# First-layer sums of the 7-product scheme kept in PSUM, GpSimd sums of weights and tokens issued steps ahead of ScalarE's copies, and the PSUM split of the balancing stage changed

## The chip, the cores and the metric

The kernel runs on one core of a Trainium2 chip. The metric is device time of one execution in microseconds (us); several executions are timed and their median is quoted. Engine names: PE is TensorE, DVE is VectorE, ACT is ScalarE, POOL is GpSimd, SP is SyncE, which issues the DMAs.

## What is computed

Three stages follow each other on 2304 tokens of 512 values (4 batches of 576), all in fp32:

```python
p_packed = sm_attn(p, k, v)              # 32 packed rows for each of 8 heads
x = sm_attn(q, p_packed, p_packed)       # 4 x 576 tokens, 512 wide
P = exp(x @ w_gate - max)                # 8 experts
for _ in range(8):                       # balancing
    P /= P.sum(1); P /= P.sum(0); P *= N / E
out = sum over e of P[:, e] * (relu(x @ w1[e]) @ w2[e])      # d_ff 1024
r = relu(out @ w_in); result = (s * r * r + b) @ w_out       # d_ff 2048
```

## The kernel before

**Precision.** PE multiplies in the fp32r format. Each operand is kept as a high part, rounded to fp32r, and a low part, the rest; a product takes three passes (high by high, high by low, low by high). Whatever feeds PE is therefore made twice: ACT casts or copies the high part, and DVE or POOL subtracts it from the full value to get the low part.

**Units.** The eight experts' first layers are cut into 32 units `u` of 256 hidden columns. Since the tokens are `x = a2 * ppf` (attention weights by packed values), the first layer is applied as `z = ppf * w1` (`zmm`, 64 small PE products a unit) and then `x`-sided weights by `z`. Units 0 to 4 run in the plain way: `mm1a` makes 288 tokens by 128 hidden columns with 6 PE matmuls of 288 columns, ACT takes the relu as the high part, DVE the low part, and `tile2` (line 478, six matmuls of 128x512 for a tile of 128 tokens) makes the second layer in a PSUM bank, which DVE weighs and adds to `acc` (line 493). The balancing iterations (`balance`) are woven between the slots of units 0 to 3 and need PSUM banks of their own. After them ACT weighs what lies in `acc` already (`gated`, line 484).

**7-product units.** Units 5 to 29 (25 of them, four batches `b` each, so 100 slots; `slotw`) compute the four blocks of a 2x2 block product with seven block products instead of eight (`mm1w`, `product`; each product is three matmuls of 288 columns into a PSUM bank). A slot uses three banks of the pool "h", which has four: `ps_a` collects products 1, 6, 5, 3 one on top of the other, `ps_b` takes product 2, `ps_e` products 7 and 4. After products 1, 6 and 5 ACT copies what `ps_a` holds to SBUF (`snap`, line 425); DVE adds a bank to such a copy (`plus`, line 428, in place in SBUF); ACT takes the relu of the sum (line 416) and DVE subtracts it for the low part of `h` (`h_put`, line 417). Between the jobs `j1` to `j4` stand the second-layer tiles of the slot before: five in slots b=0 and b=2, four in b=1 and b=3.

**What the products need.** `z_whole(u+1)` makes the next unit's `z` with 64 PE matmuls into all four banks of the pool "y", and ACT copies them to `zp` (line 374). For each batch `z_split` has POOL form four sums (line 384), ACT cast two pieces to `zz` (line 386) and POOL make their low parts (line 387). `x_sums` does the like for the tokens, once for each batch, while unit 4 runs: POOL adds high and low part to `px` (line 394), forms four differences `tp` (line 397), ACT casts them to `xt` (line 398), and POOL makes the low part (line 399). `px` and `tp` take the two buffers of the pool "w", in which the second-layer weights also lie (`load_w2`, line 116 the low part).

**Order.** Behind the attention stage, instructions are not issued as the program is written: the framework's scheduler reorders them on each engine by a cost model of its own, within the dependences and buffer counts. Where a side job is called decides only roughly where its instructions land. The lines of calls are `side` lists, in `slotw` and in the loop over `u` and `b`.

**PSUM.** Eight banks. From the end of the attention stage on, the kernel before has y=4 and h=4; balancing sums and `z` take "y" banks.

Of the kernel before, what the change touches and what calls it, by code (L numbers as in the profile page):

```python
# [25 lines left out]
HB = S // 2  # L26
# [16 lines left out]
def tile_kernel(ctx: ExitStack, tc: tile.TileContext, qT, kT, vv, pb, w1c, w2c, wcat64, wg, sv, bv, out):  # L43
# [301 lines left out]
    def zmm(u, pr, qs=(0, 1), tags="mm"):  # L345

        w = wts[1, u]
        ps = [psa(t, "ps_z") for t in tags]
        for q in qs:
            for r, c, rows, cols in heads():  # L350
                mmul(ps[r][cols, q * FU:(q + 1) * FU], ppf[rows, 2 * pr + q, cols], w[rows, c, :],  # L351
                     start=True, stop=True)
        return ps

    def zput(u, pr, ps, qs=(0, 1)):
        if (u, pr) not in zs:
# [20 lines left out]
    def z_split(u, b):  # L377

        src = zplain[0][:, b // 2, :, b % 2, :]
        zz = zq_[u, b] = z_p.tile([128, 2, 7, 128], F32R, tag="z", name="zz")  # L380
        sums = wt_p[-1].tile([128, 4, 128], F32, tag="sums", name="sums")
        for n, (x_, y_, op) in enumerate(((src[:, 0], src[:, 2], ALU.add), (sums[:, 0], src[:, 1], ALU.subtract),
                                          (src[:, 1], src[:, 0], ALU.subtract), (src[:, 3], sums[:, 1], ALU.subtract))):
            G.tensor_tensor(out=sums[:, n], in0=x_, in1=y_, op=op)  # L384
        for o, s_ in ((slice(0, 3), src[:, 1:4]), (slice(3, 7), sums)):
# [3 lines left out]
    def x_sums(b):  # L389

        o = slice(b * S, (b + 1) * S)
        px = w_p.tile([128, 2048], F32, tag="w", name="px")[:, :2 * S].rearrange("p (c t) -> p c t", c=2)
        tp = w_p.tile([128, 2048], F32, tag="w", name="tp")[:, :4 * HB].rearrange("p (n t) -> p n t", n=4)
        G.tensor_tensor(out=px, in0=xa[0][:, :, o].bitcast(F32), in1=xa[1][:, :, o].bitcast(F32), op=ALU.add)
        x11, x12, x21, x22 = px[:, 0, :HB], px[:, 0, HB:], px[:, 1, :HB], px[:, 1, HB:]
        for n, (x_, y_) in enumerate(((x12, x11), (x22, tp[:, 0]), (x22, x12), (x21, tp[:, 1]))):
            G.tensor_tensor(out=tp[:, n], in0=x_, in1=y_, op=ALU.subtract)  # L397
        A.copy(xt[0][:, b, 0], tp)
        G.tensor_tensor(out=xt[0][:, b, 1], in0=tp, in1=xt[0][:, b, 0].bitcast(F32), op=ALU.subtract)  # L399

    LEFT = {1: 0, 4: 1, 2: 2, 5: 3, 6: 4, 7: 5, 3: 6}

    def product(n, u, b, p_, start=False):

        o = b * S
        for m, (k, a) in enumerate(PASSES):
            x_ = {1: lambda: xa[k][:, 0, o:o + HB], 2: lambda: xa[k][:, 1, o:o + HB],
                  3: lambda: xa[k][:, 1, o + HB:o + S], 4: lambda: xt[0][:, b, k, 3],
                  5: lambda: xt[0][:, b, k, 0], 6: lambda: xt[0][:, b, k, 1], 7: lambda: xt[0][:, b, k, 2]}[n]()
            mmul(p_[:, :HB], zq_[u, b][:, a, LEFT[n], :], x_, start=start and m == 0, stop=m == 2,  # L410
                 skip_group_check=True)

    def h_put(b, f, t, s_):
        o = (b % 2) * S + t * HB
        hh, hl = (h[:, f, k, o:o + HB] for k in range(2))
        A.activation(out=hh, in_=s_, func=AF.Relu)  # L416
        V.scalar_tensor_tensor(out=hl, in0=s_, scalar=0.0, in1=hh.bitcast(F32), op0=ALU.max, op1=ALU.subtract)  # L417

    def mm1w(u, b):

        p, s_ = {}, {}

        def snap(n):
            s_[n] = wt_p[-1].tile([128, HB], F32, tag=f"snap{n}", name="snap")
            A.copy(s_[n], p["a"][:, :HB])  # L425

        def plus(n, bank):
            V.tensor_tensor(out=s_[n], in0=p[bank][:, :HB], in1=s_[n], op=ALU.add)  # L428

        def j1():  # L430
            p["a"], p["b"] = psa("h", "ps_a"), psa("h", "ps_b")
            product(1, u, b, p["a"], True)
            snap(1)
            product(2, u, b, p["b"], True)
            plus(1, "b")
            h_put(b, 1, 0, s_[1])

        def j2():
            p["e"] = psa("h", "ps_e")
            product(6, u, b, p["a"])  # L440
            snap(2)
            product(7, u, b, p["e"], True)

        def j3():
            product(5, u, b, p["a"])
            snap(3)
            plus(3, "e")
# [133 lines left out]
    def slotw(u, b, side=()):  # L581
# [37 lines left out]
    with tc.tile_pool(name="ppf", bufs=1) as ppf_p, tc.tile_pool(name="w1p", bufs=2) as w1_, ExitStack() as start:  # L619
# [3 lines left out]
        with tc.manual_schedule(), tc.tile_pool(name="at", bufs=1) as at_p, ExitStack() as early:  # L623
# [114 lines left out]
            for s in range(1, B - 1):  # L738
# [17 lines left out]
        share(ctx, y=4, h=4)  # L756
        banks.pop("m")
        order = [(u, 1, q) for u in range(UP) for q in (2, 3)]
        order += [(u, pr, q) for u in range(UP, W0) for pr in range(2) for q in range(4)]
        cut = order.index((UE, 0, 1))  # L760
        with tc.tile_pool(name="mid", bufs=1) as mid:
            bal = balance(mid)
            for u, pr, q in order[:cut]:
                side = []
                if u >= UP:
                    side = side1(u, pr, q)
                elif u == UP - 1:
                    side = zjobs(UP) if q == 2 else []
                elif q == 2:
                    side = [lambda: list(load_w2(UP))]  # L770
                slot1(u, pr, q, side + [nxt(bal)])
            for _ in bal:
                pass
        start.close()
        with tc.tile_pool(name="wt", bufs=1) as wt:
            wt_p.append(wt)
            xt.append(wt.tile([128, B, 2, 4, HB], F32R, name="xt"))
            for n, (u, pr, q) in enumerate(order[cut:]):
                side = side1(u, pr, q)
                if n < B:  # L780
                    side.append(lambda b=n: x_sums(b))
                if (pr, q) == (1, 0):
                    side.insert(0, lambda: z_whole(W0))
                if (pr, q) == (1, 2):
                    side.append(lambda: z_split(W0, 0))
                slot1(u, pr, q, side)
            for u in range(W0, W9):
                for b in range(B):
                    side = []
                    if b < B - 1:  # L790
                        side.append(lambda u=u, b=b: z_split(u, b + 1))
                    if b == 0:
                        side.append(lambda u=u: list(load_w2(u + 1)))
                    if b == B - 1:
                        if u + 1 < W9:
                            side += [lambda u=u: z_whole(u + 1), lambda u=u: z_split(u + 1, 0)]
                        else:
                            side += zjobs(u + 1)
                        side.append(lambda u=u: load_w1(u + 2))
# [78 lines left out]
```

## Time and profile before

| | |
|---|---|
| median of three timed runs | 1824.58 us (1822.94 to 1825.3) |
| the profiled execution: own time, span of its trace | 1825.6 us, 1823.8 us |
| busy: PE, DVE, ACT, POOL | 94%, 69%, 40%, 38% |
| mean granted TensorE clock | 0.991 of full speed |
| 7-product units | 286 to 1324 us of the span |
| the second model (two matrices and the squared relu) | from about 1410 us |

The profile is of one execution. A row of a timeline gives the start, the duration, the engine, the line, the operation with its output and inputs, and in brackets how long the engine had been idle before and what ended that. A "waits" row sums such idle time by what ended it. Matmuls are pipelined, so the modelled ends of neighbouring rows overlap. For what an engine's delay costs, the starts of repeated instructions are safer than the idle time.

### The profile page before, as it was taken

Reading aid. Unit: us, or ns where it says so; the run is one execution under the profiler, and the core shown is the slowest. Engines: PE = TensorE matmul, PEld = TensorE weight load, DVE = VectorE, ACT = ScalarE, POOL = GpSimd, SP = SyncE. Lnnn points to the kernel's source line nnn. Section 1 sums busy time; section 2 is a strip of 40 time slices with the busy share of each in tenths; the row PEclk is TensorE's granted clock in tenths of the full one; section 3 lists DMA queues with packets and bytes.
Section 4 is the critical chain, followed back from the end, with each engine's and each line's share of the span. In section 5 each row is a group of like instructions: output and inputs, shape, how many; then the busy total and the mean of one; then the engine's idle time right before and its main releaser. Section 6 shows DMA issues by size and latency. Waiting matters only on the chain.

```text
span 1823.8 us, 28626 instructions
## 1 busy us (share of the span) xinstructions
PE 1720.6 (94%) x11227; PEld 1455.6 (80%) x11227; DVE 1253.1 (69%) x2374; ACT 728.8 (40%) x1609; POOL 689.6 (38%) x847
## 2 busy tenths in 40 slices
PE   7999969999999999999999999999999999999999
PEld 4778858777777777777777777777888898999998
DVE  4745726666666666666666666666798679988874
ACT  4542333444444444444444444444423432222221
POOL 0330083444444444444444444444210233333332
PEclk9999979999999999999999999999999999999999
DMA  9420010100001000010000010001010011111102
GB/s 276 129 59 24 13 32 16 35 24 24 24 24 36 24 24 24 24 36 24 24 24 24 25 34 24 24 24 35 2 47 24 24 35 47 36 47 37 45 12 105
DMA packets 37400, 71.59 MB, mean 39 GB/s; under 512 B 3216, under 2 KB 24720, under 8 KB 37264
## 3 DMA queue, kind: packets, MB, share of 16 engines
q1 hardware_dynamic: 37264, 69.76, 13.3%
q8 instruction: 88, 1.44, 0.3%
q14 instruction: 48, 0.39, 0.1%
HBM read 65.03 MB, written 4.72 MB: 38 GB/s over the span
## 4 chain that ended last, share of the span: by engine, by line
PE 79%; DVE 9%; POOL 5%; ACT 4%; issue 2%; DMA 1%; SPq 0%; POOLq 0%; DVEq 0%; ACTq 0%
PE ps L478 50%; PE ps L505 10%; PE ps_a L410 7%; PE ps L464 4%; PE ps_e L410 4%; DVE h L417 3%; POOL sums L384 3%; DVE acc L493 2%; ACT zp L374 2%; PE ps_z L351 2%; PE ps_b L410 1%; ACT zz L386 1%; POOL tp L397 1%; DMA q__115<-qT 1%; POOL xt L399 0%
## 5 line engine op out<-in xcount | busy, mean ns | idle before, releaser
L478 PE MATMUL ps<-w,h 128*128 128x512 f32 x4296 | 1102.5, 396 | 44.9 <-DVE h L417 25.3
L478 PEld LDWEIGHTS ps<-w,h 128*128 128x128 f32 x4296 | 775.7, 189 | 199.9 <-DVE h L417 39.6
L493 DVE SCALAR_TENSOR_TENSOR acc<-ps,pm,acc 128x512 f32<-128x512 f32 x504 | 376.6, 747 | 204.3 <-PE ps L478 201.2
L417 DVE SCALAR_TENSOR_TENSOR h<-snap,h 128x288 fp32r<-128x288 f32 x300 | 225.8, 753 | 90.3 <-ACT h L416 90.3
L425 ACT COPY snap<-ps_a 128x288 f32<-128x288 f32 x300 | 120.1, 400 | 247.8 <-PE ps_a L410 245.2
L384 POOL TENSOR_TENSOR sums<-zp 128x128 f32<-128x128 f32 x200 | 93.1, 486 | 318.4 <-ACT zp L374 312.5
L416 ACT ACTIVATE h<-snap 128x288 fp32r<-128x288 f32 x300 | 133.8, 446 | 188.6 <-DVE snap L428 185.0
L387 POOL TENSOR_TENSOR zz<-zp,zz 128x384 fp32r<-128x384 f32 x100 | 102.3, 1023 | 234.3 <-ACT zz L386 234.3
L515 POOL TENSOR_TENSOR h<-g,h 128x384 fp32r<-128x384 f32 x96 | 98.5, 1026 | 221.7 <-ACT h L514 219.5
L410 PEld LDWEIGHTS ps_a<-xt,zz 128*128 128x128 f32 x600 | 100.2, 188 | 73.2 <-ACT snap L425 45.6
L410 PE MATMUL ps_a<-xt,zz 128*128 128x288 f32 x600 | 124.7, 303 | 35.4 <-ACT snap L425 35.4
L505 PE MATMUL ps<-xa,w 128*128 128x384 f32 x576 | 146.9, 336 | 0.0
L505 PE MATMUL ps<-xb,w 128*128 128x384 f32 x576 | 146.9, 335 | 0.0
L387 POOL TENSOR_TENSOR zz<-sums,zz 128x512 fp32r<-128x512 f32 x100 | 129.0, 1290 | 0.0
L428 DVE TENSOR_TENSOR snap<-ps_e,snap 128x288 f32<-128x288 f32 x200 | 90.3, 452 | 47.5 <-ACT snap L425 43.6
L410 PEld LDWEIGHTS ps_a<-xa,zz 128*128 128x128 f32 x600 | 101.6, 189 | 16.3
L464 PE MATMUL ps<-xa,z 128*128 128x288 f32 x672 | 111.7, 304 | 2.7 <-ACT xa L274 1.9
L464 PEld LDWEIGHTS ps<-xa,z 128*128 128x128 f32 x672 | 101.3, 193 | 15.3 <-ACT xa L274 3.6
L410 PE MATMUL ps_a<-xa,zz 128*128 128x288 f32 x600 | 112.4, 296 | 0.0
L410 PE MATMUL ps_e<-xt,zz 128*128 128x288 f32 x600 | 112.4, 296 | 0.0
L514 ACT CAST h<-g 128x384 fp32r<-128x384 f32 x96 | 49.4, 515 | 149.6 <-DVE g L513 149.6
L505 PEld LDWEIGHTS ps<-xa,w 128*128 128x128 f32 x576 | 105.0, 188 | 3.7
(209 smaller groups left out, 1920.8 us busy)
## 6 DMA issues: line engine op xcount, KB each, us to landing
raw<-w2c SPq DMA_DIRECT2D x32, 512.0 KB, 3.7
raw<-wcat SPq DMA_DIRECT2D x32, 512.0 KB, 3.6
acc<-kT SPq DMA_DIRECT2D x8, 576.0 KB, 8.5
out<-acc SPq DMA_DIRECT2D x18, 256.0 KB, 2.0
acc<-vv SPq DMA_DIRECT2D x5, 576.0 KB, 9.8
q__113<-qT SPq DMA_DIRECT2D x1, 576.0 KB, 10.6
q__115<-qT SPq DMA_DIRECT2D x1, 576.0 KB, 12.4
v__157<-vv SPq DMA_DIRECT2D x1, 576.0 KB, 12.9
```

The costliest lines, as they stand in the source:

```text
L384: G.tensor_tensor(out=sums[:, n], in0=x_, in1=y_, op=op)
L387: G.tensor_tensor(out=zz[:, 1, o], in0=s_, in1=zz[:, 0, o].bitcast(F32), op=ALU.subtract)
L410: mmul(p_[:, :HB], zq_[u, b][:, a, LEFT[n], :], x_, start=start and m == 0, stop=m == 2, skip_group_check=True)
L416: A.activation(out=hh, in_=s_, func=AF.Relu)
L417: V.scalar_tensor_tensor(out=hl, in0=s_, scalar=0.0, in1=hh.bitcast(F32), op0=ALU.max, op1=ALU.subtract)
L425: A.copy(s_[n], p["a"][:, :HB])
L428: V.tensor_tensor(out=s_[n], in0=p[bank][:, :HB], in1=s_[n], op=ALU.add)
L464: mmul(p_[:, :HB], z[:, a, q // 2, i, f * 128:(f + 1) * 128], xa[k][:, i, t], start=(n + i == 0), stop=(n + i == 3))
L478: mmul(y, h[:, f, a, hc:hc + 128], ws[f][k], start=(n == 0), stop=(n == 3 * UF - 1))
L493: V.scalar_tensor_tensor(out=a, in0=y, scalar=pm[:, T, u // UE:u // UE + 1], in1=a, op0=ALU.mult, op1=ALU.add)
L505: mmul(p, w[:, a, c * 128:(c + 1) * 128], x_part(k, c)[:, b * BLK:(b + 1) * BLK], start=(n == 0), stop=(n == 3 * NC - 1))
L515: G.tensor_tensor(out=hl, in0=g, in1=hh.bitcast(F32), op=ALU.subtract)
```

## The change

It has four parts.

1. `plus` writes its sum to PSUM: in `j1` onto `ps_b`, in `j3` the sum of `ps_e` and the copy goes to `ps_b`, in `j4` onto `ps_e`. `h_put` reads the bank, on ACT and on DVE. Each sum is the same.
2. `z_split` is divided: `z_add` (POOL's four sums) is called a slot ahead of `z_split`, which only casts and makes the low parts. `z_whole(u+1)` and the loads of weights move from slot b=3: `z_whole` behind the last job of b=2, `load_w2` to b=1.
3. `x_sums` is divided into `x_add` and `x_split`, the differences are formed in place in one "w" buffer, and the four batches are spread over unit 4 and the first two 7-product slots.
4. While balancing, the banks are y=3, h=2, m=3, where balancing sums and some of `z` have "m"; y=4, h=4 come behind it.

The core of the diff:

```diff
+    def z_add(u, b):
         src = zplain[0][:, b // 2, :, b % 2, :]
-        zz = zq_[u, b] = z_p.tile([128, 2, 7, 128], F32R, tag="z", name="zz")
         sums = wt_p[-1].tile([128, 4, 128], F32, tag="sums", name="sums")
...
+        z_sums[u, b] = [(slice(0, 3), src[:, 1:4]), (slice(3, 7), sums)]
+    def z_split(u, b):
+        zz = zq_[u, b] = z_p.tile([128, 2, 7, 128], F32R, tag="z", name="zz")
+        for o, s_ in z_sums[u, b]:
             A.copy(zz[:, 0, o], s_)
             G.tensor_tensor(out=zz[:, 1, o], in0=s_, in1=zz[:, 0, o].bitcast(F32), op=ALU.subtract)
...
-        px = w_p.tile([128, 2048], F32, tag="w", name="px")[:, :2 * S].rearrange("p (c t) -> p c t", c=2)
-        tp = w_p.tile([128, 2048], F32, tag="w", name="tp")[:, :4 * HB].rearrange("p (n t) -> p n t", n=4)
...
+        for out_, x_, y_ in ((x11, x12, x11), (x12, x22, x12), (x22, x22, x11), (x21, x21, x22)):
+            G.tensor_tensor(out=out_, in0=x_, in1=y_, op=ALU.subtract)
...
-    def h_put(b, f, t, s_):
+    def h_put(b, f, t, p_):
+        s_ = p_[:, :HB]
...
-        def plus(n, bank):
-            V.tensor_tensor(out=s_[n], in0=p[bank][:, :HB], in1=s_[n], op=ALU.add)
+        def plus(n, bank, to):
+            V.tensor_tensor(out=p[to][:, :HB], in0=p[bank][:, :HB], in1=s_[n], op=ALU.add)
...
-            plus(1, "b")
-            h_put(b, 1, 0, s_[1])
+            plus(1, "b", "b")
+            h_put(b, 1, 0, p["b"])
...
-            plus(3, "e")
-            h_put(b, 0, 1, s_[3])
+            plus(3, "e", "b")
+            h_put(b, 0, 1, p["b"])
...
-            plus(2, "e")
-            h_put(b, 0, 0, s_[2])
+            plus(2, "e", "e")
+            h_put(b, 0, 0, p["e"])
...
+            share(start, y=3, h=2, m=3)
             bal = balance(mid)
...
+        banks.pop("m")
+        share(ctx, y=4, h=4)
...
+            early = {(0, 1): [(x_add, 0)], (0, 3): [(x_split, 0)], (1, 0): [(x_add, 1), (z_whole, W0)],
+                     (1, 1): [(z_add, W0, 0)], (1, 2): [(x_split, 1), (z_split, W0, 0)],
+                     (1, 3): [(z_add, W0, 1), (x_add, 2)]}
...
+                    if b == 2:
+                        side[3].append((z_whole, u + 1) if u + 1 < W9 else (zrun, u + 1))
```

What the scheduler makes of it is shown at three places. First PE at a unit's change, before (u=14 to 15): `ps_2` are second-layer tiles, `zz_7487` belongs to batch b=3 of the old unit, `ps_z` are the matmuls of `z_whole`, of which one row of 64 is kept at each end.

```order
L478 MATMUL ps_2_7549<-w_6938,h_73 128x512 x6
L410 MATMUL ps_a_7557<-xa0_70,zz_7487 128x288 x2
...
L410 MATMUL ps_b_7558<-xa0_70,zz_7487 128x288 x2
...
L478 MATMUL ps_2_7570<-w_6938,h_73 128x512 x6
L351 MATMUL ps_z_7579<-w1__7265,ppf_86 32x256
...
L410 MATMUL ps_a_7557<-xt_2576,zz_7487 128x288 x3
L410 MATMUL ps_e_7619<-xt_2576,zz_7487 128x288 x3
```

and with the change (`zz_7500` is batch b=3 here):

```order
L491 MATMUL ps_2_7549<-w_7037,h_73 128x512 x6
L351 MATMUL ps_z_7558<-w1__7252,ppf_86 32x256
...
L491 MATMUL ps_2_7598<-w_7037,h_73 128x512 x6
L422 MATMUL ps_a_7606<-xa0_70,zz_7500 128x288 x2
...
L422 MATMUL ps_b_7607<-xa0_70,zz_7500 128x288 x2
...
L491 MATMUL ps_2_7619<-w_7037,h_73 128x512 x6
L422 MATMUL ps_a_7606<-xt_2588,zz_7500 128x288 x3
```

Before, product 6 (the second into `ps_a`, from `xt`) follows `z` at once; now a tile, products 1 and 2 and another tile stand between `z` and product 6.

Second, ACT at the same place, before and with the change. `zp` are the copies of `z`, `zz` the casts (the second needs POOL's sums), `snap` the copies of `ps_a`.

```order
L374 COPY zp_7578<-ps_z_7579 128x2x2x128
L374 COPY zp_7578<-ps_z_7580 128x2x2x128
L386 CAST zz_7636<-zp_7578 128x384
L386 CAST zz_7636<-sums_7637 128x512
L374 COPY zp_7578<-ps_z_7597 128x2x2x128
L374 COPY zp_7578<-ps_z_7598 128x2x2x128
L425 COPY snap_7623<-ps_a_7557 128x288
L425 COPY snap_7649<-ps_a_7557 128x288
L416 ACTIVATE h_73<-snap_7649 128x288
```

```order
L374 COPY zp_7557<-ps_z_7558 128x2x2x128
L374 COPY zp_7557<-ps_z_7559 128x2x2x128
L392 CAST zz_7668<-zp_7557 128x384
L392 CAST zz_7668<-sums_7627 128x512
L374 COPY zp_7557<-ps_z_7576 128x2x2x128
L374 COPY zp_7557<-ps_z_7577 128x2x2x128
L438 COPY snap_7611<-ps_a_7606 128x288
L429 ACTIVATE h_73<-ps_b_7607 128x288
L438 COPY snap_7636<-ps_a_7606 128x288
```

ACT's order is the same up to the first `snap`: four copies and two casts. That first `snap` was the one behind product 6 and is now the one behind product 1.

Third, ACT at the end of the balancing stage, before and with the change: `acc` is the weighing of line 484 (497 with the change), `xt` the cast of a batch's token differences, `h` relus of unit 4.

```order
L484 ACTIVATE acc_72<-acc_72,pm_78 128x512 x5
L467 ACTIVATE h_73<-ps_1_2577 128x288
L398 CAST xt_2576<-tp_2601 128x1152
L467 ACTIVATE h_73<-ps_1_2609 128x288
L398 CAST xt_2576<-tp_2637 128x1152
L467 ACTIVATE h_73<-ps_1_2627 128x288
L467 ACTIVATE h_73<-ps_1_2654 128x288
L398 CAST xt_2576<-tp_2682 128x1152
```

```order
L410 CAST xt_2588<-px_2612 128x1152
...
L410 CAST xt_2588<-px_2719 128x1152
L497 ACTIVATE acc_72<-acc_72,pm_78 128x512 x3
L480 ACTIVATE h_73<-ps_1_2589 128x288
L497 ACTIVATE acc_72<-acc_72,pm_78 128x512 x3
L480 ACTIVATE h_73<-ps_1_2618 128x288
L497 ACTIVATE acc_72<-acc_72,pm_78 128x512
L410 CAST xt_2588<-px_2912 128x1152
L410 CAST xt_2588<-px_3016 128x1152
L480 ACTIVATE h_73<-ps_1_2636 128x288
```

The casts of the first two batches now stand between weighings, and those of the last two directly behind each other, still ahead of relus of unit 4.

## Rows read from the trace of the kernel before

**Rows 1.** The page, busy time, share of the span and instructions of each engine.

```profile
PE 1720.6 (94%) x11227; PEld 1455.6 (80%) x11227; DVE 1253.1 (69%) x2374; ACT 728.8 (40%) x1609; POOL 689.6 (38%) x847
```

**Rows 2.** What PE waited for, 286 to 1324 us: total, times, longest (us).

```profile
PE ps_a L410 <- ACT snap L425: 35.4, 24, 1.8
PE ps L478 <- DVE h L417: 25.3, 50, 0.7
```

**Rows 3.** Timeline of PE, 582 to 624 us: start, duration, operation, [idle before].

```profile
584.77 0.55 PE L410 MATMUL ps_a<-xa,zz 128*128 128x288 f32 x3
...
593.08 0.56 PE L410 MATMUL ps_a<-xa,zz 128*128 128x288 f32 x3
...
593.87 0.62 PE L478 MATMUL ps<-w,h 128*128 128x512 f32 x2
...
595.12 1.21 PE L478 MATMUL ps<-w,h 128*128 128x512 f32 x4 [0.50 <-DVE h L417]
...
603.54 0.55 PE L410 MATMUL ps_a<-xa,zz 128*128 128x288 f32 x3
...
605.80 2.06 PE L351 MATMUL ps_z<-w__5677,ppf 64*32 64x256 f32 x64
...
611.72 0.66 PE L410 MATMUL ps_a<-xt,zz 128*128 128x288 f32 x3 [1.48 <-ACT snap L425]
...
615.77 0.56 PE L410 MATMUL ps_a<-xa,zz 128*128 128x288 f32 x3
```

**Rows 4.** Timeline of DVE and POOL, 591 to 595 us.

```profile
591.32 0.46 DVE L417 SCALAR_TENSOR_TENSOR h<-snap,h 128x288 fp32r<-128x288 f32 x1 [0.51 <-ACT h L416]
...
593.28 0.75 DVE L493 SCALAR_TENSOR_TENSOR acc<-ps,pm,acc 128x512 f32<-128x512 f32 x1
...
593.46 1.29 POOL L387 TENSOR_TENSOR zz<-sums,zz 128x512 fp32r<-128x512 f32 x1
...
593.95 1.12 DVE L417 SCALAR_TENSOR_TENSOR h<-snap,h 128x288 fp32r<-128x288 f32 x1
```

**Rows 5.** Instructions by tile (snap, ps_a): duration ns min/median/max, first and last start.

```profile
L417 DVE SCALAR_TENSOR_TENSOR h<-snap,h x300: 446/460/1987, 288.2 to 1321.7; 128x288 fp32r<-128x288 f32 x150
L428 DVE TENSOR_TENSOR snap<-ps_b,snap x100: 444/449/458, 287.3 to 1311.4; 128x288 f32<-128x288 f32 x100
...
L417 DVE SCALAR_TENSOR_TENSOR h<-ps_a,h x100: 446/448/458, 294.0 to 1319.9; 128x288 fp32r<-128x288 f32 x100
```

**Rows 6.** Timeline of ACT, 605 to 613 us.

```profile
609.77 0.62 ACT L386 CAST zz<-sums 128x512 fp32r<-128x512 f32 x1 [1.12 <-POOL sums L384]
610.30 1.06 ACT L374 COPY zp<-ps_z 128x512 f32<-128x512 f32 x2
611.25 0.41 ACT L425 COPY snap<-ps_a 128x288 f32<-128x288 f32 x1
```

**Rows 7.** Timeline of ACT and PE, 216 to 290 us.

```profile
218.97 0.72 ACT L484 ACTIVATE acc<-acc,pm 128x512 f32<-128x512 f32 x1 [1.74 <-DVE pm L339]
...
239.34 0.96 PE L464 MATMUL ps<-xa,z 128*128 128x288 f32 x6
244.40 2.93 PE L478 MATMUL ps<-w,h 128*128 128x512 f32 x6 [4.09 <-ACT h L467]
...
265.46 2.93 PE L478 MATMUL ps<-w,h 128*128 128x512 f32 x6 [9.14 <-ACT zp L374]
...
286.20 0.56 PE L410 MATMUL ps_a<-xa,zz 128*128 128x288 f32 x3
```

**Rows 8.** Groups by line: count, busy us, mean ns of one, idle before and releaser.

```profile
L394 POOL TENSOR_TENSOR px<-xa,xa 128x1152 f32<-128x1152 f32 x4 | 10.6, 2658 | 41.3 <-PE ps L478 41.1
L399 POOL TENSOR_TENSOR xt<-tp,xt 128x1152 fp32r<-128x1152 f32 x4 | 10.6, 2639 | 1.3 <-ACT xt L398 1.3
...
L397 POOL TENSOR_TENSOR tp<-px 128x288 f32<-128x288 f32 x8 | 6.2, 803 | 39.8 <-PE ps L478 39.6
...
L398 ACT CAST xt<-tp 128x1152 fp32r<-128x1152 f32 x4 | 4.6, 1155 | 22.4 <-POOL tp L397 22.4
```

**Rows 9.** What PE waited for, 60 to 228 us: total, times, longest (us).

```profile
PE ps L478 <- DVE z L362: 1.8, 3, 0.6
```

More of the change, by code (lines that the diff above doesn't have):

```diff
@@ L375, in z_whole @@
                        ps[pr][r].rearrange("p (q s m) -> p q s m", q=2, s=2))
-    def z_split(u, b):
+    z_sums = {}
+    def z_add(u, b):
         src = zplain[0][:, b // 2, :, b % 2, :]
-        zz = zq_[u, b] = z_p.tile([128, 2, 7, 128], F32R, tag="z", name="zz")
         sums = wt_p[-1].tile([128, 4, 128], F32, tag="sums", name="sums")
@@ L384, in z_split, with x_add, x_split @@
             G.tensor_tensor(out=sums[:, n], in0=x_, in1=y_, op=op)
-        for o, s_ in ((slice(0, 3), src[:, 1:4]), (slice(3, 7), sums)):
+        z_sums[u, b] = [(slice(0, 3), src[:, 1:4]), (slice(3, 7), sums)]
+    def z_split(u, b):
+        zz = zq_[u, b] = z_p.tile([128, 2, 7, 128], F32R, tag="z", name="zz")
+        for o, s_ in z_sums[u, b]:
             A.copy(zz[:, 0, o], s_)
             G.tensor_tensor(out=zz[:, 1, o], in0=s_, in1=zz[:, 0, o].bitcast(F32), op=ALU.subtract)
-    def x_sums(b):
+    x_plain = {}
+    def x_add(b):
         o = slice(b * S, (b + 1) * S)
-        px = w_p.tile([128, 2048], F32, tag="w", name="px")[:, :2 * S].rearrange("p (c t) -> p c t", c=2)
-        tp = w_p.tile([128, 2048], F32, tag="w", name="tp")[:, :4 * HB].rearrange("p (n t) -> p n t", n=4)
[L394 to L399, printed above, removed]
+        px = x_plain[b] = w_p.tile([128, 2048], F32, tag="w", name="px")[:, :2 * S]
+        G.tensor_tensor(out=px.rearrange("p (c t) -> p c t", c=2), in0=xa[0][:, :, o].bitcast(F32),
+                        in1=xa[1][:, :, o].bitcast(F32), op=ALU.add)
+        x11, x12, x21, x22 = (px[:, n * HB:(n + 1) * HB] for n in range(4))
+        for out_, x_, y_ in ((x11, x12, x11), (x12, x22, x12), (x22, x22, x11), (x21, x21, x22)):
+            G.tensor_tensor(out=out_, in0=x_, in1=y_, op=ALU.subtract)
+    def x_split(b):
+        px = x_plain.pop(b).rearrange("p (n t) -> p n t", n=4)
+        A.copy(xt[0][:, b, 0], px)
+        G.tensor_tensor(out=xt[0][:, b, 1], in0=px, in1=xt[0][:, b, 0].bitcast(F32), op=ALU.subtract)
     LEFT = {1: 0, 4: 1, 2: 2, 5: 3, 6: 4, 7: 5, 3: 6}
@@ L407, in product @@
             x_ = {1: lambda: xa[k][:, 0, o:o + HB], 2: lambda: xa[k][:, 1, o:o + HB],
-                  3: lambda: xa[k][:, 1, o + HB:o + S], 4: lambda: xt[0][:, b, k, 3],
-                  5: lambda: xt[0][:, b, k, 0], 6: lambda: xt[0][:, b, k, 1], 7: lambda: xt[0][:, b, k, 2]}[n]()
+                  3: lambda: xa[k][:, 1, o + HB:o + S], 4: lambda: xt[0][:, b, k, 2],
+                  5: lambda: xt[0][:, b, k, 0], 6: lambda: xt[0][:, b, k, 3], 7: lambda: xt[0][:, b, k, 1]}[n]()
             mmul(p_[:, :HB], zq_[u, b][:, a, LEFT[n], :], x_, start=start and m == 0, stop=m == 2,
                  skip_group_check=True)
-    def h_put(b, f, t, s_):
+    def h_put(b, f, t, p_):
+        s_ = p_[:, :HB]
         o = (b % 2) * S + t * HB
@@ L446, in j3 @@
             snap(3)
-            plus(3, "e")
-            h_put(b, 0, 1, s_[3])
+            plus(3, "e", "b")
+            h_put(b, 0, 1, p["b"])
         def j4():
             product(3, u, b, p["a"])
-            h_put(b, 1, 1, p["a"][:, :HB])
+            h_put(b, 1, 1, p["a"])
             product(4, u, b, p["e"])
-            plus(2, "e")
-            h_put(b, 0, 0, s_[2])
+            plus(2, "e", "e")
+            h_put(b, 0, 0, p["e"])
         return [j1, j2, j3, j4]
@@ L579, in slot1, with slotw @@
         slot(first, side, 0 if u < UP and (u, q) != (0, 2) else 1)
-    def slotw(u, b, side=()):
+    def slotw(u, b, side):
         todo, jobs = ready[:], mm1w(u, b)
         ready[:] = made(u, b // 2, 2 * (b % 2)) + made(u, b // 2, 2 * (b % 2) + 1)
-        side = list(side)
-        while jobs or todo:
-            for q_ in (jobs, todo, side):
+        for n in range(5):
+            for q_ in (jobs, todo):
                 if q_:
                     q_.pop(0)()
-        for s in side:
-            s()
+            for s in side.get(n, ()):
+                s()
     def slot2(v, b, side=()):
@@ L602, in zjobs, with zrun @@
         ps = []
-        return [lambda: ps.extend((zmm(u, 0, tags="yy"), zmm(u, 1, tags="yy"))), lambda: zput(u, 0, ps[0]),
+        t0, t1 = ("ym", "mm") if "m" in banks else ("yy", "yy")
+        return [lambda: ps.extend((zmm(u, 0, tags=t0), zmm(u, 1, tags=t1))), lambda: zput(u, 0, ps[0]),
                 lambda: zput(u, 1, ps[1])]
+    def zrun(u):
+        for job in zjobs(u):
+            job()
     def side1(u, pr, q):
@@ L755, in tile_kernel @@
                 })
-        share(ctx, y=4, h=4)
-        banks.pop("m")
         order = [(u, 1, q) for u in range(UP) for q in (2, 3)]
@@ L777, in tile_kernel @@
             xt.append(wt.tile([128, B, 2, 4, HB], F32R, name="xt"))
[L778 to L786, printed above, removed]
+            early = {(0, 1): [(x_add, 0)], (0, 3): [(x_split, 0)], (1, 0): [(x_add, 1), (z_whole, W0)],
+                     (1, 1): [(z_add, W0, 0)], (1, 2): [(x_split, 1), (z_split, W0, 0)],
+                     (1, 3): [(z_add, W0, 1), (x_add, 2)]}
@@ L787, in tile_kernel @@
+            for u, pr, q in order[cut:]:
+                slot1(u, pr, q, side1(u, pr, q) + [lambda f=f, a=a: f(*a) for f, *a in early.get((pr, q), [])])
             for u in range(W0, W9):
                 for b in range(B):
[L789 to L799, printed above, removed]
@@ L800, in tile_kernel @@
-                    slotw(u, b, side)
+                    v, c = (u, b + 1) if b + 1 < B else (u + 1, 0)
+                    w, d = (u, b + 2) if b + 2 < B else (u + 1, b + 2 - B)
+                    side = {0: [], 1: [], 2: [], 3: [], 4: []}
+                    if u == W0 and b < 2:
+                        side[2].append((x_split, b + 2))
+                        if b == 0:
+                            side[4].append((x_add, 3))
+                    if b + 1 < B:
+                        side[0].append((z_split, u, b + 1))
@@ new lines, in tile_kernel @@
+                    if b + 2 < B:
+                        side[3].append((z_add, u, b + 2))
+                    if b == 2:
+                        side[3].append((z_whole, u + 1) if u + 1 < W9 else (zrun, u + 1))
+                    if b == 3 and u + 1 < W9:
+                        side[0].append((z_add, u + 1, 0))
+                        side[2].append((z_split, u + 1, 0))
+                        side[4].append((z_add, u + 1, 1))
+                    if b == 3:
+                        side[1].append((load_w1, u + 2))
@@ L801, in tile_kernel @@
+                    if b == 1:
+                        side[1].append((lambda v: list(load_w2(v)), u + 1))
+                    slotw(u, b, {n: [lambda f=f, a=a: f(*a) for f, *a in fs] for n, fs in side.items()})
         with tc.tile_pool(name="mid2", bufs=1) as mid:
```

## The prediction

> **What bounds the kernel now.** I began with the busy times on the page: PE works in 94% of the span and no other engine in more than 69% [rows 1]. So time is to be gained only where PE stands, and the next view is what PE waits for. In the 1038 us of the 7-product units it has two waits, always the same [rows 2]: 24 times for the copy `snap` of what `ps_a` holds (35.4 us), and 50 times for the low part of `h` (25.3 us). What a wait costs is read better from the starts of product 1 in PE's timeline [rows 3] than from idle time, since matmul ends are modelled. A slot of four tiles without a wait lasts 593.08 - 584.77 = 8.31 us. It holds 21 matmuls of 288 columns and 24 of 512, 18336 columns, so 0.453 ns a column and 1.39 us for a tile of six. The next slot has five tiles and should last 9.70; it lasts 10.46, a loss of **0.76** for a wait shown as 0.50. The one after it has four tiles and some 2.0 us of `z`, should last 10.31 and lasts 12.23, a loss of **1.92** for a wait shown as 1.48. A unit has two slots of the five-tile kind and one with `z`: 3.44 us are lost in its 41.5. Over 50 and 24 such places that is 38 + 46 = **84 us**, the most that the units can give.
>
> **Why PE waits for h.** The timelines of DVE and POOL at 593 us [rows 4] show it. DVE's low-part instruction on `snap` starts at 593.95 and takes 1.12 us instead of its median of 0.46 [rows 5]; it stays in work until POOL's 1.29 us subtraction, begun at 593.46, ends. The same instruction on `ps_a` never took over 0.458 in 100 cases, the one on `snap` up to 1.987 [rows 5]: with two operands in SBUF it is held up while POOL works, with one in PSUM it is not.
>
> **Part 1, sums in PSUM.** All three sums of a slot now reach ACT and DVE from a bank. I take 0.448 for the low part [rows 5]. It then ends at 593.95 + 0.45 = 594.40, and PE hears of it 0.05 later, as it did before (595.07 to 595.12). PE would ask at 593.87 + 2 x 0.23 + 0.13 = 594.46 (two matmuls of the tile and one pass of product 6 stand ahead). So the wait is gone but for what weight loads need ahead of a matmul; I leave 0.07 and take 0.69 of the 0.76: 50 x 0.69 = **34.5 us**.
>
> [...]
>
> What the trace has no row for is a DVE instruction that writes to PSUM. From below, it could be quicker than the 0.449 of the same sum written to SBUF [rows 5], and then nothing more is gained, since PE would not wait there anyway. From above I have no row of that kind; the nearest long one of DVE is its 0.75 for 512 columns with `acc` [rows 4]. I take 0.45, the same operands and the same 288 columns. At 0.75 a slot has 3 x 0.3 = 0.9 us more on DVE, of which it has some 3.0 free (last rivals, below), but the low part that is just in time comes 0.3 later where the sum stands right ahead of it: up to 50 x 0.3 = 15 us lost. ACT's copies and relus keep their count, and it is at 40% [rows 1].
>
> A new wait comes with it: `ps_b` is used again in `j3`, so product 2 of the next slot must wait for that low part. It ended at 591.32 + 0.46 = 591.78 [rows 4]; product 2 is at 593.08 + 0.40 = 593.48. 1.7 us of slack: nothing.
>
> **Part 2, z a slot earlier.** Before, ACT copies two of the four `z` banks, casts, then waits 1.12 us for POOL's sums, casts them (609.77), copies two more banks (610.30) and only then makes the `snap` behind product 6 (611.25 to 611.66) [rows 6], for which product 5 stands until 611.72 [rows 3]. Counted from the start of `z`, at 605.80 [rows 3], that first `snap` is done after 5.9 us. ACT's order is the same with the change, and POOL's four sums start at the first copies as before: `z_add` of batch 0 stands behind `z`, not ahead of it, so ACT's chain is not shorter. What changes is PE's: the first `snap` is now the one behind product 1, which product 6 needs, and between `z` and product 6 stand a tile, products 1 and 2 and another tile, 1.39 + 0.79 + 1.39 = 3.57 us of work behind the 2.0 of `z`. PE asks 5.57 us after the start of `z`; before it asked after 611.72 - 1.48 - 605.80 = 4.44 [rows 3]. The wait falls from 1.48 to about 0.36, and with a restart I leave 0.6 lost instead of 1.92: 1.33 gained, 24 x 1.33 = **31.9 us**. If all of it went it would be 46, and if nothing does, 0.
>
> The last unit's `z` is written as before by ACT and DVE (`zrun`), now right ahead of a tile. Such a tile waited 0.6 us each of three times earlier on [rows 9]: **-0.5 us**.
>
> **Parts 3 and 4, before the units.** From 239.34 to the first product at 286.20 PE does ten halves of a first layer (0.80 each: six of 288 columns), eleven tiles and `z`: 8.0 + 15.3 + 2.0 = 25.3 us, and takes 46.9 [rows 7]. [...] With the change ACT's cast of the first batch stands behind the first weighings (from 218.97 [rows 7]), so it is at about 222; POOL's low part (2.6), the second batch's sums (2.7 + 4 x 0.8 = 5.9) and cast (1.2) and low part (2.6) then reach 234.7, and batches 3 and 4 together (11.7) 246.5; durations from [rows 8]. Two casts stand ahead of the next relu, which comes at about 247.6 where it came at 243.94, so PE's first wait grows to some 8 us. The second, 9.14, was for copies of `z` behind the fourth cast and two weight casts that waited for a low part; it goes, but for a few us. I set the loss with the change at about 14 and the gain at **7 us**; ends: 0, and 21.6. In the balancing stage `z` had to share banks with the tiles; with banks of its own the 1.8 us [rows 9] go, **2 us** with the restarts.
>
> **Sum.** 34.5 + 31.9 - 0.5 + 7 + 2 = 74.9 us. Against the profiled execution's own 1825.6 us that gives 1750.7; the median of the three runs is 1.0 lower, so the forecast is **1750 us**. Everything else has the same instructions.
>
> **Rivals.**
> - *The front gives nothing*: the four batches' sums still stand ahead of relus, and PE loses as much as now. 1750 + 9 = 1759. For it: ACT's two casts in a row ahead of a relu. Chance 0.15.
> - *The wait for `snap` stays*, though moved: if ACT's casts of `zz` wait longer for POOL's sums than before, since POOL has more queued there, product 6 waits as long as now. 1750 + 32 = 1782. Against it: 3.6 us of PE's work lie between. 0.08.
> - *The wait for h stays*: DVE's low part from `ps_e` still comes late, because the sum into PSUM is slower, or because it is still held up by POOL. 1750 + 34.5 = 1784. Against it: 100 instructions from `ps_a`, of at most 0.458. 0.07.
> - *DVE becomes the bound, and the kernel is slower.* In a slot DVE has three sums of duration a, four low parts (4 x 0.45) and 4.5 additions to `acc` (4.5 x 0.75): 3a + 5.2 us, where PE needs 38.0 / 4 = 9.5. Now a is 0.45. From a = 1.43 on DVE sets the pace, and beyond a = 1.72 a slot is longer than the 10.37 of before. At a = 2.0, near the longest instruction on `snap`, 100 slots of 11.2 instead of 10.37 cost 83 us: 1825 + 83 - 9 = 1899. For it: no row shows a write to PSUM by DVE. Against it: reads from PSUM cost nothing extra, and nothing of this kind is as slow. 0.04.
> - *The change does nothing there*: the sums were already in time and the waits are set by something else, such as the tile's own bank. 1825. Against it: the waits' releasers and the 1.12. 0.02.
>
> **How the numbers follow.** My forecast has 0.64: 1741 to 1762, by the z wait gone wholly (-8), the front's ends and a slower sum (+12). The first rival lies within. 8 in 10 reach from 1738 (z wait gone and most of the front) to 1776 (h or z half left, the front without gain). About 0.2%, 3.6 us, is what a measurement of this kernel can tell from no change; the three rivals before the slower one all gain more, so faster is 0.94, same 0.02, slower 0.04.
>
> **What would show it.** In the profile after: low parts `h<-ps_e` and `h<-ps_b` at 0.45 with no long ones; sums into `ps_b` and `ps_e` near 0.45; the row "PE ps <- DVE h" of the units down from 25.3 us to a few; "PE ps_a <- ACT snap" down from 35.4 to 5 to 12; a unit's period from 41.5 to about 38.7 us; the first product at about 277. I am wrong if the sums take over 0.75, if the period stays above 40, or if PE's clock row falls below 9 inside the units.

## The result and the profile after

| | before | changed |
|---|---|---|
| median of the timed runs | 1824.94 us (1822.94 to 1825.36) | 1748.86 us (1748.17 to 1750.04) |
| ratio to before | | 0.9586, 95% interval 0.9569 to 0.9602 |
| the profiled execution: own time, span | 1825.6 us, 1823.8 us | 1750.04 us, 1748.3 us |

The forecast was 1750 us, the range 1738 to 1776 us. The page's busy times, as in [rows 1]; PE works 98% of a span that is 75.5 us shorter:

```profile
PE 1707.2 (98%) x11227; PEld 1451.8 (83%) x11227; DVE 1172.8 (67%) x2374; ACT 715.4 (41%) x1609; POOL 681.7 (39%) x847
```

What PE waits for in the 7-product units (276 to 1250 us: total, times, longest), to be held against [rows 2]:

```profile
PE ps_a L422 <- ACT snap L438: 2.6, 17, 0.2
PE ps L491 <- DVE z L362: 0.6, 1, 0.6
```

Of 60.7 us, 3.2 are left. The wait for h is not on the list any more; the 0.6 is the last unit's `z`, which the sum had at -0.5. PE's timeline over one unit (as [rows 3]):

```profile
567.63 0.55 PE L422 MATMUL ps_a<-xa,zz 128*128 128x288 f32 x3
...
576.15 2.01 PE L351 MATMUL ps_z<-w__5664,ppf 64*32 64x256 f32 x64
...
579.60 0.56 PE L422 MATMUL ps_a<-xa,zz 128*128 128x288 f32 x3
...
582.06 0.66 PE L422 MATMUL ps_a<-xt,zz 128*128 128x288 f32 x3
...
588.29 0.55 PE L422 MATMUL ps_a<-xa,zz 128*128 128x288 f32 x3
...
598.05 0.55 PE L422 MATMUL ps_a<-xa,zz 128*128 128x288 f32 x3
...
606.37 0.55 PE L422 MATMUL ps_a<-xa,zz 128*128 128x288 f32 x3
```

Five of these, the `ps_a<-xa` rows, are product 1 of a slot (the row at 582.06 reads `xt` and is product 6). The slots last 11.97 (five tiles and `z`; 11.70 without any wait), 8.69 (four tiles; 8.31), 9.76 (five; 9.70) and 8.32 us, together 38.74 where a unit took 41.5. The five-tile loss fell from 0.76 to 0.06. What is left around `z` is 0.27 + 0.38 = 0.65 of 1.92, as the sum had it (0.6). ACT's row for the `snap` that product 6 needs:

```profile
581.60 0.41 ACT L438 COPY snap<-ps_a 128x288 f32<-128x288 f32 x1
```

It ends 5.9 us after the start of `z` (576.15), as the first `snap` did before: ACT's chain is no shorter, and PE asks for its end later.

DVE and POOL at the place of [rows 4]:

```profile
567.84 0.75 DVE L506 SCALAR_TENSOR_TENSOR acc<-ps,pm,acc 128x512 f32<-128x512 f32 x1 [0.29 <-PE ps L491]
...
568.01 1.29 POOL L393 TENSOR_TENSOR zz<-sums,zz 128x512 fp32r<-128x512 f32 x1
...
568.50 0.45 DVE L430 SCALAR_TENSOR_TENSOR h<-ps_e,h 128x288 fp32r<-128x288 f32 x1
```

The same three instructions stand in the same order, at the same distances, and POOL's takes the same 1.29 us. Only the low part is 0.45 instead of 1.12. By tile (ps_b and ps_e; duration ns min/median/max):

```profile
L430 DVE SCALAR_TENSOR_TENSOR h<-ps_b,h x200: 447/457/459, 282.8 to 1245.3; 128x288 fp32r<-128x288 f32 x100
L441 DVE TENSOR_TENSOR ps_b<-ps_b,snap x100: 454/466/467, 281.9 to 1240.1; 128x288 f32<-128x288 f32 x100
L441 DVE TENSOR_TENSOR ps_b<-ps_e,snap x100: 466/467/467, 286.2 to 1244.4; 128x288 f32<-128x288 f32 x100
...
L441 DVE TENSOR_TENSOR ps_e<-ps_e,snap x100: 455/456/456, 288.2 to 1246.7; 128x288 f32<-128x288 f32 x100
...
L430 DVE SCALAR_TENSOR_TENSOR h<-ps_e,h x100: 446/448/458, 289.6 to 1248.2; 128x288 fp32r<-128x288 f32 x100
```

None of 300 low parts is over 0.459, though 149 of them ran beside a POOL instruction. That answers the price for which no row stood: a sum written to PSUM takes 0.456 to 0.467 us, against 0.449 written to SBUF [rows 5].

Before the units, PE's waits from 228 to 290 us are one group, and the timeline of ACT and PE shows its largest:

```profile
PE ps L491 <- ACT h L480: 9.8, 3, 7.5
```

```profile
222.85 2.55 ACT L497 ACTIVATE acc<-acc,pm 128x512 f32<-128x512 f32 x4
...
250.26 2.21 ACT L410 CAST xt<-px 128x1152 fp32r<-128x1152 f32 x2 [8.38 <-POOL px L405]
...
252.83 1.65 PE L491 MATMUL ps<-w,h 128*128 128x512 f32 x3 [7.53 <-ACT h L480]
...
280.84 0.55 PE L422 MATMUL ps_a<-xa,zz 128*128 128x288 f32 x3
```

ACT stands in front of two token casts for 8.38 us, and PE for the relu behind them. From the first weighing to the first product it is 58.0 us; before, 67.2 [rows 7]. In both traces PE's granted clock behind these long waits is 0.50 of full speed: the three matmuls at 252.83 took 1.65 us, and in the kernel before the six behind each of the waits of 4.09 and 9.14 took 2.93 [rows 7]. In the units, at a granted clock of 1.00, a tile's six take 1.39. This execution came to the weighing 3.9 us later, at 222.85: it lost this in the attention stage, whose code is the same, where among others its wait for the DMA of the first weights was 1.6 us instead of 0.6. So the first product was at 280.84 and not at 277; in the profiles of two runs below that leave the stretch before the units as it is here (part 1 undone, `z_whole` back in b=3) it was at 275.99 and 276.82.

### The profile page after: what moved, and what is told of

Its sections match the earlier page's. It is cut to its first block, busy times and chain, and to the rows that moved or that the text cites. A ratio compares the mean times of both kernels' runs of the same rounds, so it can differ in the third digit from the quotient of the medians.

```text
span 1748.3 us, 28772 instructions
## 1 busy us (share of the span) xinstructions
PE 1707.2 (98%) x11227; PEld 1451.8 (83%) x11227; DVE 1172.8 (67%) x2374; ACT 715.4 (41%) x1609; POOL 681.7 (39%) x847
## 4 chain that ended last, share of the span: by engine, by line
PE 83%; ACT 5%; POOL 5%; DVE 4%; issue 2%; DMA 1%; SPq 0%; POOLq 0%; DVEq 0%; ACTq 0%
PE ps L491 50%; PE ps L518 10%; PE ps_a L422 9%; PE ps_e L422 5%; PE ps L477 4%; POOL sums L385 3%; PE ps_z L351 2%; ACT zp L374 2%; PE ps_b L422 2%; DMA w__117<-w1c 1%; ACT zz L392 1%; POOL px L405 0%; POOL xt L411 0%; POOL px L401 0%; ACT snap L438 0%
## 5 line engine op out<-in xcount | busy, mean ns | idle before, releaser
L385 POOL TENSOR_TENSOR sums<-zp 128x128 f32<-128x128 f32 x200 | 88.0, 460 | 219.9 <-ACT zp L374 214.0
L430 DVE SCALAR_TENSOR_TENSOR h<-ps_b,h 128x288 fp32r<-128x288 f32 x200 | 91.3, 456 | 83.8 <-ACT h L429 83.8
L429 ACT ACTIVATE h<-ps_b 128x288 fp32r<-128x288 f32 x200 | 82.3, 411 | 113.2 <-DVE ps_b L441 113.2
L142 POOL TENSOR_TENSOR w<-m,w 128x256 fp32r<-128x256 f32 x64 | 48.4, 756 | 144.2 <-ACT w L141 144.2
```

## The experiments

Times are medians; each is set against the 1748.86 us of the changed kernel or the kernel before beside it (1824.87, 1825.72 and 1825.09 us). The kernel before moved by up to 0.8 us between these sets (it was at 1824.94 beside the changed kernel), so a difference of about 1 us is not read as one.

### Part 1: which sum, and why

**All three sums in PSUM, nothing else.** The kernel before with the `plus` and `h_put` of the change.

> The kernel before with part 1 alone (all three sums into PSUM, low parts read the bank). My theory: the low part with both operands in SBUF is held up while GpSimd works, and that alone makes the 50 waits for h. Then 50 x 0.69 = 34.5 us go: about 1790 us, the wait of PE for DVE's h below 3 us, the 24 waits for snap unchanged at about 35 us, no low part of h over 0.47 us. Rival (the parts of the change need each other, DVE is late for other reasons): 1805 us or more, and waits for h of 10 us or more.

Measured 1791.66 us, ratio 0.9812 (0.9798 to 0.9827): 33.2 us. PE's wait for `snap`, and the group of low parts with the longest mean (count, busy us, mean ns, idle before):

```profile
PE ps_a L410 <- ACT snap L426: 36.0, 24, 1.5
```

```profile
L418 DVE SCALAR_TENSOR_TENSOR h<-ps_b,h 128x288 fp32r<-128x288 f32 x200 | 91.3, 457 | 84.3 <-ACT h L417 84.3
```

The wait for h is gone from the list, and the one for `snap` stands as it was. The rival, that the parts need each other, falls.

**The change without part 1.** The same lines the other way round.

> The changed kernel with part 1 undone (sums and low parts in SBUF again). My theory: the parts add up, so the waits for h come back whole: 1749 + 34.5 = about 1783 us, PE's wait for DVE's h about 25 us, low parts up to 2 us long. Rival (GpSimd's sums being made earlier already keep it away from the low parts): below 1765 us.

Measured 1782.43 us, 33.6 above the changed kernel. PE's wait, and the low parts by tile:

```profile
PE ps L490 <- DVE h L429: 24.7, 50, 0.7
```

```profile
L429 DVE SCALAR_TENSOR_TENSOR h<-snap,h x300: 447/462/1995, 278.0 to 1277.3; 128x288 fp32r<-128x288 f32 x150
```

The 50 waits return, and low parts of up to 2 us with them. Part 1 is worth 33 us from either side.

**The last sum of a slot alone.**

```diff
-            plus(2, "e")
-            h_put(b, 0, 0, s_[2])
+            V.tensor_tensor(out=p["e"][:, :HB], in0=p["e"][:, :HB], in1=s_[2], op=ALU.add)
+            h_put(b, 0, 0, p["e"][:, :HB])
```

> The kernel before with only the last of the three sums of a slot (the one onto ps_e, job j4) in PSUM. My theory: only the low part behind this sum is on PE's path, since the other two are long done when a tile asks for them: nearly the whole gain, 1790 to 1794 us, though the other low parts stay long (up to 2 us). Rival (all three low parts delay DVE's queue together): a third of the gain, about 1813 us.

Measured 1791.28 us, 33.6 us below before: all of part 1, by one sum of three. The wait for h is gone, though 200 low parts are still made from SBUF; 48 of them took over 0.55 us, up to 1.88:

```profile
L417 DVE SCALAR_TENSOR_TENSOR h<-snap,h x200: 457/459/1877, 289.9 to 1284.4; 128x288 fp32r<-128x288 f32 x100
```

**The first two sums alone.** The same edit at `j1` and `j3`, the last sum in SBUF.

> The kernel before with the first two sums of a slot (onto ps_b, jobs j1 and j3) in PSUM, and the last in SBUF as before. My theory: no gain, 1821 to 1828 us, PE's wait for DVE's h stays at about 25 us in 50 places, though 200 of the 300 low parts are short now. Rival (all three count): two thirds of the gain, about 1802 us.

Measured 1825.61 us, ratio 1.0001 (0.9991 to 1.0010). PE's wait, and the low parts that are still made from SBUF:

```profile
PE ps L478 <- DVE h L417: 25.2, 50, 0.7
```

```profile
L417 DVE SCALAR_TENSOR_TENSOR h<-snap,h x100: 448/1118/1397, 297.9 to 1322.7; 128x288 fp32r<-128x288 f32 x100
```

The low parts of the first two sums are no longer held up (0.457 us on average; 48 of their 200 were in the run above), and nothing was gained. The low part of the last sum is the only one that a tile asks for in the moment it ends. Its median is 1.118 us here, and it is held up in 74 of 100 slots.

No run takes POOL's work alone away, but the trace of the kernel before shows POOL beside every long low part and not only at 593 us. Of the 298 low parts on `snap` with a timeline row of their own, 120 took over 0.55 us, and each had POOL instructions running beside it for at least 0.5 us; of the 178 short ones two had more than 0.05 us of POOL beside them. Of the 100 low parts on `ps_a`, 73 had, and none took over 0.458.

### Part 2: TensorE's work, or sums made ahead

**`z_whole` back in slot b=3.** The sums stay a step ahead.

```diff
-                    if b == 2:
-                        side[3].append((z_whole, u + 1) if u + 1 < W9 else (zrun, u + 1))
+                    if b == 3:
+                        side[0].append((z_whole, u + 1) if u + 1 < W9 else (zrun, u + 1))
```

> The changed kernel with z_whole called behind the first job of slot b=3 again; GpSimd's sums stay a step ahead of the casts. ScalarE's order around z is the same in both (two copies, two casts, two copies, snap); on TensorE the tile and products 1 and 2 lie ahead of z again. My theory: the 24 waits for snap come back, since what went was TensorE's work between z and product 6: 1749 + 24 x 1.27 = about 1779 us, the wait about 1.4 us each. Rival (the sums made ahead are what counts): at most 1755 us.

Measured 1780.95 us, 32.1 above the changed kernel. The wait of [rows 2] is back:

```profile
PE ps_a L422 <- ACT snap L438: 35.8, 24, 1.8
```

**No sums ahead.** `z_add` is called right before `z_split`, for every batch; `z_whole` stays where the change put it.

```diff
...
                     if b + 1 < B:
-                        side[0].append((z_split, u, b + 1))
-                    if b + 2 < B:
-                        side[3].append((z_add, u, b + 2))
+                        side[0] += [(z_add, u, b + 1), (z_split, u, b + 1)]
...
-                        side[0].append((z_add, u + 1, 0))
-                        side[2].append((z_split, u + 1, 0))
-                        side[4].append((z_add, u + 1, 1))
+                        side[2] += [(z_add, u + 1, 0), (z_split, u + 1, 0)]
```

> The changed kernel with z_add called right ahead of z_split again (no sums a step ahead), z_whole where the change put it. My theory: the sums made ahead do nothing for the time, since GpSimd has idle time between batches and batch 0 of a unit cannot be ahead of z anyhow: 1747 to 1753 us. Rival (casts now wait for GpSimd at every batch): ScalarE's relus come 0.5 us or more late 75 times, 1770 us or more.

Measured 1747.9 us (1747.17 to 1751.06), the same as the changed kernel. The cast that needs the sums, here and in the changed kernel (count, busy us, mean ns, idle before):

```profile
L392 ACT CAST zz<-sums 128x512 fp32r<-128x512 f32 x100 | 62.0, 620 | 27.8 <-POOL sums L385 27.8
```

```profile
L392 ACT CAST zz<-sums 128x512 fp32r<-128x512 f32 x100 | 61.8, 618 | 27.6 <-POOL sums L385 27.6
```

ACT waits for POOL's sums as long in both: 1.1 us once a unit, in batch 0, whose sums follow `z` at once. So dividing `z_split` is worth nothing; where `z` stands in PE's order is worth 32 us.

### Parts 3 and 4

**Four banks each for y and h while balancing, as before.** `share(ctx, y=4, h=4)` and `banks.pop("m")` stand ahead of the balancing loop again.

> The changed kernel with part 4 undone (four banks for y and four for h while balancing, balancing sums and z in y banks). My theory: the three waits of tiles for z come back, 1.8 us and restarts: 1750 to 1752 us. Rival (fewer banks for tiles and halves cost as much as the separate ones gain): 1747 to 1749 us.

Measured 1754.06 us, 5.2 above the changed kernel. PE's waits from 60 to 290 us:

```profile
PE ps L491 <- ACT h L480: 12.2, 4, 6.8
PE ps L491 <- DVE z L362: 1.8, 3, 0.6
```

The three waits for `z` are those of [rows 9]. But part 4 gives more than these: the waits for relus before the units are 2.4 us longer as well, so it is worth 5, where theory and rival had 1 to 3 and 0. Most of it lies in that stall, not in the balancing: from the first weighing to the first product this run takes 62.5 us, the changed kernel 58.0. The wait behind the longest one is where they part (ACT and PE, this run first, then the changed kernel):

```profile
256.99 1.05 ACT L115 CAST w<-raw 128x1024 fp32r<-128x1024 f32 x1 [1.52 <-POOL xt L411]
258.39 1.65 PE L491 MATMUL ps<-w,h 128*128 128x512 f32 x3 [3.67 <-ACT h L480]
```

```profile
255.11 0.40 ACT L480 ACTIVATE h<-ps 128x288 fp32r<-128x288 f32 x1
255.56 1.65 PE L491 MATMUL ps<-w,h 128*128 128x512 f32 x3 [1.09 <-ACT h L480]
```

Here ACT makes a second weight cast, for which it waits 1.52 us, ahead of the relu; in the changed kernel that relu stands ahead of the cast. Why the scheduler orders them so with these banks was not tried.

**Token sums as before.** `x_sums` of the kernel before, called in the first four slots of unit 4.

> The changed kernel with part 3 undone (x_sums in two buffers, all four batches called at the start of the last plain unit). My theory: the casts of tokens and weights again stand ahead of z's copies and the wait of about 9 us for them returns: 1749 + 9 = about 1758 us, the first product at 289 to 291 us of the span. Rival (the waits are set by GpSimd's total work, which is the same): 1747 to 1752 us.

Measured 1752.95 us, 4.1 above the changed kernel: between theory (9) and rival (at most 3). PE's waits, again from 60 to 290 us:

```profile
PE ps_z L351 <- DVE acc L500: 7.2, 1, 7.2
PE ps L485 <- ACT h L474: 6.3, 2, 3.9
```

13.5 us of waits instead of 9.8. The theory was right on ACT and wrong on PE. ACT's cast of the fourth batch is late again, at 259.40 (260.01 in the kernel before), and the casts stand ahead of relus and of `z`'s copies. But the tile's wait of 9.14 for those copies didn't return. PE stands in the middle of `z` instead, for a bank that DVE's weighing frees, behind one of those relus:

```profile
263.01 1.96 PE L351 MATMUL ps_z<-w__2407,ppf 64*32 64x256 f32 x30 [7.24 <-DVE acc L500]
```

The first product came at 283.49, not at 289 to 291: 64.5 us after the first weighing, against 67.2 before and 58.0 in the changed kernel. So part 3 shortens the stall in front of the units and doesn't remove it. In this run and the one before it no time lies within the changed kernel's 1748.17 to 1750.04, so both differences are clear of the noise, though their size is good to 1 us only.

The five undone pieces are 33.6 + 32.1 - 1.0 + 5.2 + 4.1 = 74.0 us; the whole change is 76.1. The parts add up to within some 2 us.

### A faster version

**Two of `z`'s four copies on VectorE.** What is left around `z` was laid to ACT's chain of copies and casts.

```diff
-                A.copy(zp[:, pr, 2 * r:2 * r + 2].rearrange("p s q m -> p q s m"),
...
+                (V.tensor_copy if pr else A.copy)(zp[:, pr, 2 * r:2 * r + 2].rearrange("p s q m -> p q s m"),
...
```

> The changed kernel with the last two of z's four copies to zp made by VectorE, which stands idle there for 2.4 us, instead of ScalarE. My theory: what is left of the wait for snap (0.15 shown, 0.6 lost by the starts, 24 times) is ScalarE's chain of four copies and two casts; 1.07 us less in it puts snap ahead of TensorE's demand: 1749 - 24 x 0.5 = about 1737 us. Rival (the loss there is not ScalarE's but comes with z itself, or VectorE's copies delay the next sums): 1747 us or more.

Measured 1738.58 us (1738.31 to 1739.14), ratio to before 0.9520 (0.9506 to 0.9535): 10.3 us below the changed kernel. The wait for `snap` is not on the list any more: it comes at 574.79, 4.5 us after the start of `z` at 570.29 instead of 5.45. ACT's row and PE's timeline:

```profile
574.79 0.39 ACT L438 COPY snap<-ps_a 128x288 f32<-128x288 f32 x1
```

```profile
561.78 0.55 PE L422 MATMUL ps_a<-xa,zz 128*128 128x288 f32 x3
...
570.29 2.01 PE L351 MATMUL ps_z<-w__5664,ppf 64*32 64x256 f32 x64
...
573.74 0.56 PE L422 MATMUL ps_a<-xa,zz 128*128 128x288 f32 x3
...
582.06 0.55 PE L422 MATMUL ps_a<-xa,zz 128*128 128x288 f32 x3
```

The slot behind `z` lasts 8.32, so its 0.38 are gone. The slot with `z` still lasts 11.96, so 0.26 of the loss comes with `z` itself, and not from ACT (or `z` costs 2.26 and not the 2.0 taken for it): the rival was right in that part.

**Token sums of batches 1 to 3 on VectorE.**

```diff
-        G.tensor_tensor(out=px.rearrange("p (c t) -> p c t", c=2), in0=xa[0][:, :, o].bitcast(F32),
...
+        E_ = V if b else G
+        E_.tensor_tensor(out=px.rearrange("p (c t) -> p c t", c=2), in0=xa[0][:, :, o].bitcast(F32),
...
-            G.tensor_tensor(out=out_, in0=x_, in1=y_, op=ALU.subtract)
+            E_.tensor_tensor(out=out_, in0=x_, in1=y_, op=ALU.subtract)
```

> The changed kernel with the token sums of batches 1 to 3 made by VectorE instead of GpSimd. My theory: TensorE's waits of 9.8 us in the last plain unit are ScalarE's casts behind GpSimd's sums (5.9 us for a batch); with these off GpSimd the casts come in time and most of the wait with its slow restarts goes: about 1740 us. Rival (VectorE's own instructions are held up by GpSimd's low parts and tiles wait instead): 1746 to 1752 us.

Measured 1744.16 us (1743.84 to 1746.48), ratio to before 0.9553 (0.9538 to 0.9568): 4.7 us, about half of what was expected. PE's waits from 200 to 272 us, DVE's sums in its timeline, and all twelve by tile (duration ns min/median/max):

```profile
PE ps L492 <- DVE h L482: 2.1, 1, 2.1
PE ps L492 <- ACT zp L374: 1.2, 1, 1.2
PE ps L492 <- DVE acc L505: 0.7, 1, 0.7
PE ps L492 <- ACT h L481: 0.2, 1, 0.2
```

```profile
239.72 0.44 DVE L406 TENSOR_TENSOR px<-px 128x288 f32<-128x288 f32 x1
...
241.85 3.31 DVE L406 TENSOR_TENSOR px<-px 128x288 f32<-128x288 f32 x2
...
246.11 2.56 DVE L406 TENSOR_TENSOR px<-px 128x288 f32<-128x288 f32 x1
```

```profile
L406 DVE TENSOR_TENSOR px<-px x12: 442/447/2833, 228.7 to 246.1; 128x288 f32<-128x288 f32 x12
```

The 9.8 us of waits for relus went and 4.2 others are left, half of them for a low part of DVE. The rival had named such delays: a subtraction of 288 columns from SBUF takes 0.44 us here, or up to 2.83. That POOL was at work beside the long ones is an inference from part 1; none of these rows shows it.

**Both.**

> Both of the last two: the two places are 10 us or more apart, so the gains add: about 1728 us. Rival: if either is refuted, what the other gives alone.

Measured 1733.64 us (1731.72 to 1736.76), ratio to before 0.9494 (0.9477 to 0.9511): 15.2 us below the changed kernel, where the two alone give 10.3 + 4.7 = 15.0. The gains add, as the theory said; the 1728 is missed because the token sums gave half of what was expected. It is the fastest of all.

## Why the prediction was right

- **The bound.** Reading losses from the starts of product 1 gave 0.76 and 1.92 where idle time showed 0.50 and 1.48. The runs confirm the larger figures: part 1 brought 33.2 and 33.6 us, and 25.3 was all that the waits showed; part 2 and the run on `z`'s copies together brought 32.1 + 10.3 = 42.4 us, where the waits had shown 35.4.
- **Part 1** was forecast at 34.5 and is 33 us. The last sum of a slot makes all of it, as the chain 593.95 to 595.12 in [rows 3] and [rows 4] said; the other two sums make nothing. The bound of 0.75 for a sum into PSUM wasn't needed: it is 0.46. The slack of the new wait, product 2 for the low part of `ps_b`, held.
- **Reads from PSUM** cost a low part nothing extra, as the prediction said against its slower rival: 0.446 to 0.459 us from PSUM in the changed kernel, and at least 0.446, with a median of 0.460, from SBUF before [rows 5].
- **Part 2** was forecast at 31.9 and is 32.1 us, by the mechanism named: PE's 3.6 us of work between `z` and product 6. The wait left is 2.6 us in all, below the 5 to 12 that was named as the sign. ACT's chain is as long as before (5.9), as the step said. The sums made ahead are worth nothing; the step had said so of batch 0.
- **Parts 3 and 4** were forecast at 7 + 2 and are 4.1 + 5.2. Both terms were mis-sized, and that their errors cancel is luck. By place they were off the other way. The 7 us stood for the stretch from the first weighing to the first product (of the 46.9 - 25.3 = 21.6 us lost in its part from 239.34 on, 14 were to stay): it fell from 67.2 to 58.0 us, by 9.2. The 2 us stood for the balancing: from a cast of `z` in it (before, then with the change) to the first weighing at 218.97 and 222.85 it took 94.7 us and then 94.4, though the three waits for `z` are gone.

```profile
124.25 2.06 ACT L361 CAST z<-ps_z 128x512 fp32r<-128x512 f32 x4 [0.49 <-PE ps_z L351]
```

```profile
128.47 2.06 ACT L361 CAST z<-ps_z 128x512 fp32r<-128x512 f32 x4 [0.49 <-PE ps_z L351]
```

So the term for the banks had the wrong place: they count mostly in the stall in front of the units, where the step put nothing down to them. In that stall the step was right on the order of ACT's work: the last two casts came 27.4 us after the first weighing (27.5 by the working), and the long wait was 7.53 where some 8 stood.

- **The rivals.** The front gave something, 4.1 and 5.2 us. The waits for `snap` and for h didn't stay, and DVE, at 67%, is no bound; with a = 0.46 it is far from 1.43.

## What to carry to other kernels

Before cutting waits, ask for each whether an engine asks for that result in the moment it ends: of three low parts that were held up in some of the slots, one was worth 33 us and two nothing. A wait at the end of another engine's chain can be hidden by moving the waiting engine's own work in between, with the chain as long as before; here a tile and two products more were worth 32 us, and issuing another engine's sums early nothing. Shortening the chain on top of that gave 10 more; shortening it alone was not tried. Measure what a stall costs by the distance of repeated instructions, as idle time showed two thirds to three quarters of it.

## What was not expected of the hardware

A wait cost PE more than the idle time that the profile shows: 0.76 for 0.50, and 1.92 for 1.48. VectorE's subtraction of 288 columns in SBUF took up to 2.83 us in the run with the token sums of batches 1 to 3 on VectorE, over six times its 0.44; the longest low part of before had been 1.99.
